# A scheduler that takes its due times backwards from TensorE's list, with fewer opening transfers and an add moved to ScalarE

## The chip, the cores and the metric

The kernel runs on one core of a Trainium2 chip. The metric is the device time of one execution in microseconds (us), the median of several runs. TensorE (PE) multiplies matrices, VectorE (DVE), ScalarE (ACT) and GpSimd (POOL) work elementwise, and SyncE (SP) issues the DMAs. Each engine executes its own list of instructions in order; between engines they wait on semaphores.

## The reference

33280 tokens (8 sequences of 4160) of width 192 go through a convolution of 7 taps, with weights of each token and head from a softmax, and then through a layer of 768 hidden features, each the largest of three products.

```
w = exp(weight_gen - max(weight_gen, axis=-1))          # 8 heads x 7 taps
w = w / (sum(w, axis=-1) + 1e-09)
x = einsum('bshk,bskhg->bshg', w, x_unf)                # the last 7 tokens, 8 heads of 24
h = maximum(maximum(x @ w1, x @ w2), x @ w3)            # 192 -> 768
return h @ w_out                                        # 768 -> 192
```

All is float32.

## The kernel before

The tokens are cut into 65 chunks of 512 (4 tiles of 128); two chunks make a super, for which x (`xt`) and the tap weights (`wt`) are loaded by one DMA each. For every chunk these steps follow one another:

- *Softmax of a super*: largest of the taps on DVE (L326), difference on POOL (L331), exp on ACT (L335), sum on DVE (L340), the 1e-9 added on DVE (L344), reciprocal on DVE (L348), product on POOL (L352).
- *Taps*: for each tile POOL writes the products (`r`, L370), and DVE sums them over the taps (`acc`, L382).
- *Turning*: features must lie on the partitions. DVE transposes in blocks of 32x32 (L421), and ACT moves the blocks into place with 24 copies per chunk (`room`, L432). The first two chunks are transposed on PE instead (L402).
- *Parts*: x is split in a high part of reduced precision (`xa_hi` L444, `xc` L449 on ACT) and a low part (`xa_lo` L460, `xb` L465), so that products of parts add up to float32.
- *Up*: PE computes x(w2-w1) and x(w3-w1) for six blocks `j` of 128 hidden features, two banks for each `j` (i = 0, 1), 9 matmuls of 512 columns per bank. The array's rows are used as two halves, "L" and "U". For each `j`, ACT takes max(bank, 0) of the first bank (`m`, L859), DVE the larger of that and the second bank (L867), ACT the high part (`h_hi`, L871), and DVE, or POOL for j = 1 and 4, the low part (`h_lo`, L878).
- *Down*: h @ w_out, four banks per chunk (one for each tile) of 30 matmuls, which read `h_hi` and `h_lo` of all six `j` in turn, and `wca`, `wcb`, in which w1 @ w_out is composed (casts on ACT L759, differences on DVE L767). ACT copies half a bank (`ob`, L928), DVE adds (`o`, L935), and a DMA stores the chunk.

On PE the order is written by hand: the "down" of chunk c-1 stands in chunk c behind its j = 0, 1, 2. Both kinds of matmul have line 802. So between two "down"s PE computes j = 3, 4, 5 of one chunk and j = 0, 1, 2 of the next.

The other engines' order comes from a plan (`Plan`). It plays the program through with a cost for each task: whenever an engine is free, it takes from its ready tasks the one with the earliest due time, and the program is then written in that order, which nothing changes later. Before the change a due time is a number given by hand for each task, counted from the chunk's place on PE (`needed`, a period of 21 us) or from PE's own clock of slots.

In the opening the weights are loaded and split too (Abs L573 on ACT, integer steps L579 to L604 on DVE; differences L631, L661 and low parts `wa_lo` L643 and `wb_lo` L673 on POOL; high parts L637 and L684 on ACT), while chunk 0 waits for them. SP issues nearly all DMAs; in the opening four are issued by ACT.

Of the kernel before, what the change touches and what calls it, by code (L numbers as in the profile page):

```python
# [20 lines left out]
class Hold:  # L21


    def __init__(self, pool):
        self.pool, self.users, self.taken, self.tile = pool, 0, False, None


class Task:
    def __init__(self, engine, cost, emit, deps, due, holds, end):
        self.engine, self.cost, self.emit, self.due = engine, cost, emit, due  # L30
        self.holds, self.after = holds, []
        self.end = cost if end is None else end
        self.missing = 0
        for d in deps:
            d.after.append(self)
            self.missing += 1
        for h in holds:
            h.users += 1


class Plan:
# [4 lines left out]
    LATENCY = 0.12  # L46

    def __init__(self, pools):
        self.free = dict(pools)
        self.waiting = {"L": [], "U": []}  # L50
        self.tasks = []

    def add(self, engine, cost, emit, deps=(), due=0.0, holds=(), end=None):
# [3 lines left out]
        if engine in self.FIXED:  # L57
            self.waiting[engine].append(t)
        return t

    def order(self):
        ready, busy, events, done = {}, {}, [], []
        at = dict.fromkeys(self.FIXED, 0)
        for t in self.tasks:
            ready.setdefault(t.engine, [])
            busy.setdefault(t.engine, 0.0)
            if t.missing == 0 and t.engine not in self.FIXED:
                heapq.heappush(ready[t.engine], (t.due, t.n, t))

        def can(t):  # L70
            need = {}
            for h in t.holds:
                if not h.taken:
                    need[h.pool] = need.get(h.pool, 0) + 1
            return all(self.free[p] >= n for p, n in need.items())

        def start(t, now):
            for h in t.holds:
                if not h.taken:
                    h.taken = True  # L80
                    self.free[h.pool] -= 1
# [3 lines left out]
            heapq.heappush(events, (now + t.cost, 0, t.n, t, "free"))  # L85
            heapq.heappush(events, (now + t.end, 1, t.n, t, "given"))
            heapq.heappush(events, (now + t.end + self.LATENCY, 2, t.n, t, "seen"))

        now = 0.0
        while True:  # L90
            for e in ready:
                if busy[e] > now + 1e-9:
                    continue
                if e in self.FIXED:
                    k = at[e]
                    if k < len(self.waiting[e]):
                        t = self.waiting[e][k]
# [16 lines left out]
            while events and events[0][0] <= now + 1e-9:  # L114
                _, _, _, t, what = heapq.heappop(events)
                if what == "given":
                    for h in t.holds:
                        h.users -= 1
                        if h.users == 0:
                            self.free[h.pool] += 1  # L120
                elif what == "seen":
# [9 lines left out]
def lightconv_maxout_kernel(  # L131
# [100 lines left out]
    plan = Plan(counts | {"conv": 3})  # L232
# [26 lines left out]

    def needed(c):  # L260
        return FIRST + PERIOD * c
# [4 lines left out]
    def transfer(cost, emit, deps=(), due=0.0, holds=(), on="SP"):  # L266
        issue = plan.add(on, 0.45, emit, deps, due, holds)
        return plan.add("DMA", cost, lambda: None, [issue], due, holds, end=cost + 2.0)
# [4 lines left out]
    def load_super(s):  # L273
# [3 lines left out]
        due = needed(cs[0]) - 40  # L277

# [10 lines left out]
        w = transfer(0.0005 * n * H * K, weights, (), due, [hw])  # L289
        if a >= PAD:  # L290
            t = [transfer(0.0005 * (n + PAD) * D, tokens, (), due + 0.1, [hx])]
        else:
            z = PAD - a
            zero = plan.add(
                "DVE", 1.1, lambda: pin(nc.vector.memset(buf(hx)[:, :z], 0.0)), (), due, [hx]
            )
            t = [transfer(0.0005 * (n + a) * D, tokens, (), due + 0.1, [hx])]
            for b in range(B):
                on = "ACT" if s == 0 and b % 2 else "SP"

                def rows(b=b, on=on):
                    to = slice(b * PB + 1, (b + 1) * PB)
                    q = nc.scalar if on == "ACT" else nc.sync
                    pin(
                        q.dma_start(
                            out=buf(hx)[to, :z], in_=xf[to.start - 1 : to.stop - 1, NT - z :]
                        )
                    )

                t.append(transfer(0.1, rows, [zero], due + 0.2, [hx], on))  # L310
# [5 lines left out]
    def softmax(s):  # L316
        n = len(supers[s]) * TC
        due = needed(supers[s][0]) - 32
# [8 lines left out]
            [loads[s][0]], due, [hr, hw],  # L327
# [4 lines left out]
            [a], due + 1, [hr, hw],  # L332
# [3 lines left out]
            [b], due + 2, [hw],  # L336
# [4 lines left out]
            [c], due + 3, [hd, hw],  # L341
        )
        e = plan.add(
            "DVE", 0.3, lambda: pin(nc.vector.tensor_scalar_add(part(hd), part(hd), 1e-9)),  # L344
            [d], due + 3, [hd],
        )
        f = plan.add(
            "DVE", 0.6, lambda: pin(nc.vector.reciprocal(part(hd), part(hd))), [e], due + 3, [hd]  # L348
# [4 lines left out]
            [f], due + 4, [hd, hw],  # L353
# [5 lines left out]
    def taps(c):  # L359
# [3 lines left out]
        due = needed(c)  # L363
        sums = []
        for t in range(TC):
            hr = hold("r")

            def product(t=t, hr=hr):
                pin(
# [11 lines left out]
            def total(t=t, hr=hr):  # L381
                pin(nc.vector.tensor_reduce(buf(ha)[:, t], buf(hr), axis=AX.X, op=ALU.add))  # L382

            p = plan.add(
                "POOL", 2.75, product, [ready[s], *loads[s][1]], due - 26 + 3 * t, [hr, hx, hw]
            )
            sums.append(plan.add("DVE", 1.55, total, [p], due - 22 + 3 * t, [hr, ha]))
        return ha, sums

    def blocks(c, ha, sums, wait):  # L390


        due = needed(c)
        if c < ON_TENSOR:
            ba, bb = hold("bank"), hold("bank")
            got = []
            for t in range(TC):
# [7 lines left out]
                got.append(plan.add("L", 0.6, turn, [sums[t], *wait], due, [ba, bb, ha], end=0.9))  # L405
# [4 lines left out]
        def places():  # L410
# [10 lines left out]
            "DVE", 0.97, lambda: pin(nc.vector.transpose(places()[2], buf(ha))), sums, due - 12,  # L421
# [3 lines left out]
        for q, f in enumerate(range(0, D, 32)):  # L425
            for p in range(0, P, 32):

                def move(f=f, p=p):
# [3 lines left out]
                    pin(nc.scalar.copy(to[:, :, p : p + 32], b[p : p + 32, :, f : f + 32]))  # L432

                got.append(plan.add("ACT", 0.296, move, [turned], due - 11 + q, [hv]))
        return [hv], lambda: places()[:2], got

    def parts(c, hs, places, got):
        due = needed(c)
# [5 lines left out]
            "ACT", act(CH), lambda: pin(nc.scalar.copy(buf(ah), places()[0])), of_a, due - 3,  # L444
# [5 lines left out]
                due - 2.5, [k, *hs],  # L450
# [7 lines left out]
        def a_low():  # L458
            pin(
# [3 lines left out]
        def b_low():  # L463
            pin(
# [5 lines left out]
        lo = plan.add(name, cost, a_low, [hi], due - 1.5, [al, ah, *hs])  # L470
        bl = plan.add(name, cost, b_low, cs, due - 1.4, [b, k, *hs])
# [35 lines left out]
    w_due = lambda jp, i: FIRST + 4 * jp + 2 * i  # L507

    a_in, b_in, d_in = {}, {}, {}

    def load_a(jp):
        for i, w in enumerate(words[:3]):
# [8 lines left out]
                (), w_due(jp, 0) - 22, [a_hold(jp)],  # L521
            )

    def load_b(jps):
        got = []
        for i, w in enumerate(words[:3]):
            for odd, h in enumerate(halves):
                got.append(
                    transfer(
                        0.3 * len(jps),  # L530
                        lambda i=i, w=w, odd=odd, h=h: pin(
                            nc.sync.dma_start(  # L532
                                out=raw_b()[h, jps[0] : jps[-1] + 1, i].rearrange(
                                    "p j n w -> p j (n w)"
                                ),
                                in_=w[P:].rearrange("p (j o n) -> p j o n", j=NP, o=2)[
                                    :, jps[0] : jps[-1] + 1, odd
                                ],
                            )
                        ),  # L540
                        (), w_due(jps[0], 0) - 21.5, [hraw[2]],
                    )
                )
        for jp in jps:
# [487 lines left out]
```

## Time and profile before

| | us |
|---|---|
| median of 3 runs | 1441.08 (1439.87 to 1443.25) |
| the profiled execution | 1444.6 |
| its span, first to last instruction | 1442.8 |
| mean granted clock of TensorE | 0.987 |

Durations below are of the profiled execution. In the page's second part the span is cut into 40 slices of 36 us. The first digit of each row is the opening; from the third slice on each row hardly changes.

```profile
PE   2889999999999999999999999999999999999999
DVE  7867777777777787777778777877877677777543
ACT  3547878878877887787788778877888887788773
POOL 6769888778877887887788778778877877787421
PEclk9679999999999999999999999999999999999999
```

A row gives the busy share in tenths; the PEclk row gives the clock that TensorE was granted, in tenths of full speed. Times in a chain, timeline or window count from the start of the span.

### The profile page before, as it was taken

Reading aid. Unit: us, or ns where it says so; the run is one execution under the profiler, and the core shown is the slowest. Engines: PE = TensorE matmul, PEld = TensorE weight load, DVE = VectorE, ACT = ScalarE, POOL = GpSimd, SP = SyncE. Lnnn points to the kernel's source line nnn. Section 1 sums busy time; section 2 is a strip of 40 time slices with the busy share of each in tenths; the row PEclk is TensorE's granted clock in tenths of the full one; section 3 lists DMA queues with packets and bytes.
Section 4 is the critical chain, followed back from the end, with each engine's and each line's share of the span. In section 5 each row is a group of like instructions: output and inputs, shape, how many; then the busy total and the mean of one; then the engine's idle time right before and its main releaser. Section 6 shows DMA issues by size and latency. Waiting matters only on the chain.

```text
span 1442.8 us, 37119 instructions
## 1 busy us (share of the span) xinstructions
PE 1402.0 (97%) x14878; PEld 1366.1 (95%) x14878; DVE 1043.4 (72%) x1433; ACT 1117.3 (77%) x2828; POOL 1104.2 (77%) x609
## 2 busy tenths in 40 slices
PE   2889999999999999999999999999999999999999
PEld 1579999999999999999999999999999999999998
DVE  7867777777777787777778777877877677777543
ACT  3547878878877887787788778877888887788773
POOL 6769888778877887887788778778877877787421
PEclk9679999999999999999999999999999999999999
DMA  7102111111111111111011111101111111110000
GB/s 249 46 1 79 57 68 57 68 68 57 68 46 46 57 68 68 68 57 64 28 57 68 68 68 57 68 25 67 57 68 68 57 68 44 48 57 24 23 21 26
DMA packets 23405, 85.08 MB, mean 59 GB/s; under 512 B 2768, under 2 KB 9544, under 8 KB 19136
## 3 DMA queue, kind: packets, MB, share of 16 engines
q1 hardware_dynamic: 23112, 82.44, 15.5%
q8 instruction: 116, 1.90, 0.5%
q14 instruction: 57, 0.47, 0.1%
q10 hardware_dynamic: 120, 0.28, 0.1%
HBM read 57.15 MB, written 25.56 MB: 57 GB/s over the span
## 4 chain that ended last, share of the span: by engine, by line
PE 95%; POOL 1%; DMA 1%; ACT 1%; SPq 1%; DVE 1%; issue 0%; POOLq 0%
PE bank L802 95%; POOL r L370 1%; DMA xt<-in_x_dram 1%; SPq L532 1%; DVE den L344 0%; ACT room L432 0%; DMA raw<-in_moe_w_dram 0%; SPq L516 0%; PE bank L733 0%; ACT m L859 0%; POOL wa_lo L643 0%; PE bank L731 0%; ACT wb_hi L684 0%; DVE acc L382 0%; ACT bank L573 0%
## 5 line engine op out<-in xcount | busy, mean ns | idle before, releaser
L370 POOL TENSOR_TENSOR r<-xt,wt 128x1344 f32<-128x1344 f32 x260 | 727.1, 2845 | 143.2 <-DVE acc L382 142.9
L802 PE MATMUL bank<-wo,h_hi 64*128 64x384 f32 x3120 | 675.0, 357 | 0.0
L802 PE MATMUL bank<-wo,h_lo 64*128 64x192 f32 x3120 | 603.4, 249 | 0.0
L432 ACT COPY room<-room 32x128 f32<-32x128 f32 x1512 | 448.4, 297 | 79.0 <-DVE room L421 55.9
L802 PEld LDWEIGHTS bank<-wo,h_lo 64*128 64x128 f32 x3120 | 493.0, 188 | 0.0
L802 PEld LDWEIGHTS bank<-wo,h_hi 64*128 64x128 f32 x3120 | 489.2, 186 | 0.0
L802 PE MATMUL bank<-xa_hi,wa_hi 64*128 64x512 f32 x1560 | 479.9, 394 | 6.0 <-ACT wa_hi L637 3.4
L802 PE MATMUL bank<-xa_hi,wa_lo 64*128 64x512 f32 x1560 | 477.9, 390 | 3.4 <-POOL wa_lo L643 3.3
L802 PE MATMUL bank<-xa_lo,wa_hi 64*128 64x512 f32 x1560 | 476.8, 391 | 0.5 <-DVE xa_lo L460 0.5
L382 DVE TENSOR_REDUCE acc<-r 128x192 f32<-128x1344 f32 x260 | 399.8, 1538 | 0.6 <-POOL r L370 0.3
L859 ACT ACTIVATE m<-bank 128x512 f32<-128x512 f32 x390 | 234.5, 601 | 71.4 <-PE bank L802 66.7
L935 DVE TENSOR_TENSOR o<-bank,ob 128x192 f32<-128x192 f32 x260 | 92.4, 356 | 268.7 <-ACT ob L928 268.5
L802 PE MATMUL bank<-xb,wb_hi 64*128 64x512 f32 x780 | 284.5, 390 | 0.3 <-DVE xb L465 0.3
L802 PE MATMUL bank<-xc,wb_hi 64*128 64x512 f32 x780 | 281.1, 390 | 0.2 <-ACT wb_hi L684 0.2
L802 PEld LDWEIGHTS bank<-xa_hi,wa_hi 64*128 64x128 f32 x1560 | 255.3, 186 | 13.5 <-ACT wa_hi L637 4.3
L802 PEld LDWEIGHTS bank<-xa_hi,wa_lo 64*128 64x128 f32 x1560 | 255.3, 186 | 11.2 <-POOL wa_lo L643 5.6
L802 PEld LDWEIGHTS bank<-xa_lo,wa_hi 64*128 64x128 f32 x1560 | 254.9, 187 | 6.4 <-DVE xa_lo L460 1.5
L802 PE MATMUL bank<-xc,wb_lo 64*128 64x512 f32 x780 | 258.0, 389 | 0.0
L867 DVE TENSOR_TENSOR bank<-bank,m 128x512 f32<-128x512 f32 x260 | 179.0, 689 | 42.2 <-PE bank L802 24.3
L878 POOL TENSOR_TENSOR h_lo<-m,h_hi 128x512 fp32r<-128x512 f32 x130 | 171.7, 1321 | 40.0 <-ACT h_hi L871 39.9
L802 PE MATMUL bank<-wca,xa_hi 64*128 64x384 f32 x520 | 183.4, 353 | 0.0
L878 DVE TENSOR_TENSOR h_lo<-bank,h_hi 128x512 fp32r<-128x512 f32 x260 | 172.4, 681 | 11.4 <-ACT h_hi L871 11.2
(79 smaller groups left out, 2012.5 us busy)
## 6 DMA issues: line engine op xcount, KB each, us to landing
xt<-in_x_dram SPq DMA_DIRECT2D x31, 1344.0 KB, 5.8
out_dram<-o SPq DMA_DIRECT2D x64, 384.0 KB, 2.3
wt<-in_weight_gen_dram SPq DMA_DIRECT2D x32, 224.0 KB, 2.6
h_hi<-in_moe_w_dram SPq DMA_DIRECT2D x6, 256.0 KB, 2.9
xt<-in_x_dram SPq DMA_DIRECT2D x1, 1152.0 KB, 5.8
h_lo<-in_moe_w_dram SPq DMA_DIRECT2D x6, 128.0 KB, 4.0
raw<-in_moe_w_dram SPq DMA_DIRECT2D x3, 256.0 KB, 3.6
room<-in_moe_w_out_dram SPq DMA_DIRECT2D x2, 384.0 KB, 6.4
```

Source lines behind the costliest of these rows:

```text
L370: nc.gpsimd.tensor_tensor(buf(hr).rearrange("p (h g) k -> p k h g", g=G), buf(hx)[:, la + t : la + t + K].rearrange("p k (h g) -> p k h g" ...
L382: pin(nc.vector.tensor_reduce(buf(ha)[:, t], buf(hr), axis=AX.X, op=ALU.add))
L432: pin(nc.scalar.copy(to[:, :, p : p + 32], b[p : p + 32, :, f : f + 32]))
L532: nc.sync.dma_start(out=raw_b()[h, jps[0] : jps[-1] + 1, i].rearrange("p j n w -> p j (n w)"), in_=w[P:].rearrange("p (j o n) -> p j o n", ...
L802: ins = nc.tensor.matmul(buf(hb)[:, :n], w()[h], v()[h], start=half == 0 and first, stop=half == 1 and last,)
L859: lambda: pin(nc.scalar.activation(buf(hm), buf(hb), AF.Relu)), [made], due,
L867: lambda: pin(nc.vector.tensor_tensor(buf(keep), buf(hb), buf(hm), op=ALU.max)),
L878: eng.tensor_tensor(buf(hl)[:, j], buf(keep), buf(hh)[:, j].bitcast(F32), op=ALU.subtract)
L935: nc.vector.tensor_tensor(buf(ho)[:, t], buf(hb)[:, :D], buf(hq), op=ALU.add)
```

## The change

Five things change:

1. *Due times.* A task no longer has a due time of its own, except on PE and a few others. `start_by` goes through the tasks backwards: a task must begin before the earliest of its followers, less its own duration and a latency. What PE must have when comes from its list of slots, `clock[0]`.
2. *Costs.* `vec`, `act` and `gps` get other constants; the end of a task lies a `LAG` of its engine behind the time for which it keeps the engine. A room copy is priced at .207 instead of .296, a product at 2.6 instead of 2.75, a sum at 1.455 instead of 1.55, a transpose at .86 instead of .97.
3. *Transfers of the opening.* The first tokens of each sequence need rows of the one before; these were eight DMAs of 15 rows for each of two supers, and are now four strided ones (64, 32, 16 and 8 rows) on SP. The weights' rows beyond 128 come in 6 DMAs instead of 12. The plan lets 8 transfers be under way at once.
4. *The 1e-9* is added on ACT by an activation with a bias.
5. `tokens(c)` and the "up" and "down" calls are written in another form, with the same order on PE.

```diff
-    LATENCY = 0.12
+    LATENCY = 0.1
+
+    LAG = {"DVE": 0.09, "ACT": 0.1, "POOL": 0.05}
...
+    def start_by(self):
+
+        for t in reversed(self.tasks):
+            latest = [a.by - self.LATENCY - t.end for a in t.after]
+            if t.due is not None:
+                latest.append(t.due)
+            t.by = min(latest, default=1e6)
...
-                            heapq.heappush(ready[a.engine], (a.due, a.n, a))
+                            heapq.heappush(ready[a.engine], (a.by, a.n, a))
...
     def vec(n):
-        return 0.15 + 0.00105 * n
+        return 0.062 + 0.00104 * n
     def act(n):
-        return 0.18 + 0.00084 * n
+        return 0.08 + 0.00083 * n
     def gps(n):
-        return 0.1 + 0.0024 * n
-    PERIOD = 21.0
+        return 0.12 + 0.0022 * n
...
-            for b in range(B):
-                on = "ACT" if s == 0 and b % 2 else "SP"
...
+            step = 2
+            while step <= PB:
+
+                def rows(step=step):
+                    to = buf(hx)[step // 2 :: step, :z]
+                    of = xf[step // 2 - 1 :: step, NT - z :][: P // step]
+                    pin(nc.sync.dma_start(out=to, in_=of))
...
         e = plan.add(
-            "DVE", 0.3, lambda: pin(nc.vector.tensor_scalar_add(part(hd), part(hd), 1e-9)),
-            [d], due + 3, [hd],
+            "ACT", 0.25,
+            lambda: pin(nc.scalar.activation(part(hd), part(hd), AF.Copy, bias=1e-9)),
+            [d], None, [hd],
...
-                got.append(plan.add("ACT", 0.296, move, [turned], due - 11 + q, [hv]))
+                got.append(plan.add("ACT", 0.207, move, [turned], None, [hv]))
...
-        begun, before = {}, []
+        begun, before, at = {}, [], clock[0]
...
-                    "LU"[half], slot, emit, [*deps, *(before if first else [])], 0,
+                    "LU"[half], slot, emit, [*deps, *(before if first else [])], at,
                     [hb, *holds], end=end,
                 )
+                at += slot
```

The lines of the instructions after the change: room copy L438 (before L432), `m` L854, `max` L862, `h_hi` L866, `h_lo` L873, sums L389, products L377, transpose L427, matmuls L797, `wca` and `wcb` L754 and L762, the 1e-9 L352.

**The steady part, on ACT.** This is a stretch between two "down"s about the middle of the program, before the change, from the `m` of j = 3 to the `h_hi` of j = 5 and of the next j = 0 (the row of two):

```order
960 L859 ACTIVATE m<-bank 128x512
961 L432 COPY room<-room 32x4x32 x2
962 L859 ACTIVATE m<-bank 128x512
963 L871 CAST h_hi<-bank 128x512
964 L432 COPY room<-room 32x4x32 x3
965 L859 ACTIVATE m<-bank 128x512
966 L432 COPY room<-room 32x4x32 x2
967 L871 CAST h_hi<-m 128x512
968 L432 COPY room<-room 32x4x32
969 L859 ACTIVATE m<-bank 128x512
970 L432 COPY room<-room 32x4x32 x2
971 L871 CAST h_hi<-bank 128x512 x2
```

The same stretch after the change, in every second chunk, behind the `m` of j = 3 (row 953); the last row is the `h_hi` of j = 5:

```order
954 L438 COPY room<-room 32x4x32 x7
955 L854 ACTIVATE m<-bank 128x512
956 L438 COPY room<-room 32x4x32
957 L866 CAST h_hi<-bank 128x512
958 L438 COPY room<-room 32x4x32 x4
959 L854 ACTIVATE m<-bank 128x512
960 L438 COPY room<-room 32x4x32 x4
961 L866 CAST h_hi<-m 128x512
962 L438 COPY room<-room 32x4x32
963 L854 ACTIVATE m<-bank 128x512
964 L438 COPY room<-room 32x4x32 x4
965 L866 CAST h_hi<-bank 128x512
```

Before the change 10 room copies stand between those two instructions, after it 21 in this stretch and 15 in the chunks between. The copies that stood behind the `h_hi` and among the outputs have moved up.

**The same stretch on DVE**, before the change, from the transpose to the two `h_lo` of j = 5 and the next j = 0:

```order
545 L421 STREAM_TRANSPOSE room<-acc 128x768
546 L867 TENSOR_TENSOR bank<-bank,m 128x512
547 L382 TENSOR_REDUCE acc<-r 128x192
548 L878 TENSOR_TENSOR h_lo<-bank,h_hi 128x512
549 L867 TENSOR_TENSOR m<-bank,m 128x512
550 L382 TENSOR_REDUCE acc<-r 128x192
551 L867 TENSOR_TENSOR bank<-bank,m 128x512 x2
552 L382 TENSOR_REDUCE acc<-r 128x192
553 L878 TENSOR_TENSOR h_lo<-bank,h_hi 128x512 x2
```

And after it:

```order
533 L427 STREAM_TRANSPOSE room<-acc 128x768
534 L389 TENSOR_REDUCE acc<-r 128x192
535 L862 TENSOR_TENSOR bank<-bank,m 128x512
536 L389 TENSOR_REDUCE acc<-r 128x192
537 L873 TENSOR_TENSOR h_lo<-bank,h_hi 128x512
538 L862 TENSOR_TENSOR m<-bank,m 128x512
539 L389 TENSOR_REDUCE acc<-r 128x192
540 L862 TENSOR_TENSOR bank<-bank,m 128x512 x2
541 L389 TENSOR_REDUCE acc<-r 128x192
542 L873 TENSOR_TENSOR h_lo<-bank,h_hi 128x512 x2
```

The `max` of j = 5 and of the next j = 0, a sum and the two `h_lo` stand in the same order; one more sum stands ahead of them.

**The end of the opening, on DVE**, where `wca` and `wcb` are made. Before the change:

```order
108 L767 TENSOR_TENSOR wca<-bank,wca 128x192
109 L382 TENSOR_REDUCE acc<-r 128x192
110 L344 TENSOR_SCALAR den<-den 128x64
111 L767 TENSOR_TENSOR wcb<-bank,wcb 128x192
112 L348 RECIPROCAL den<-den 128x64
```

After it:

```order
93 L356 RECIPROCAL den<-den 128x64
94 L762 TENSOR_TENSOR wca<-bank,wca 128x192
95 L347 TENSOR_REDUCE den<-wt 128x64
96 L356 RECIPROCAL den<-den 128x64
97 L762 TENSOR_TENSOR wcb<-bank,wcb 128x192
```

Between `wca` and `wcb` stood a sum of products and the 1e-9; now a sum of the softmax and a reciprocal stand there, and the 1e-9 is on ACT.

More of the change, by code (lines that the diff above doesn't have):

```diff
@@ L45, with add @@
     FIXED = ("L", "U")
-    LATENCY = 0.12
+    LATENCY = 0.1
+    LAG = {"DVE": 0.09, "ACT": 0.1, "POOL": 0.05}
     def __init__(self, pools):
-        self.free = dict(pools)
-        self.waiting = {"L": [], "U": []}
+        self.pools = dict(pools)
+        self.fixed = {"L": [], "U": []}
         self.tasks = []
-    def add(self, engine, cost, emit, deps=(), due=0.0, holds=(), end=None):
+    def add(self, engine, cost, emit, deps=(), due=None, holds=(), end=None):
+        end = cost + self.LAG.get(engine, 0.0) if end is None else end
         t = Task(engine, cost, emit, list(deps), due, list(holds), end)
@@ L57, in add @@
         if engine in self.FIXED:
-            self.waiting[engine].append(t)
+            self.fixed[engine].append(t)
         return t
+    def start_by(self):
[4 more added lines that the diff above has]
+            t.by = min(latest, default=1e6)
     def order(self):
+        self.start_by()
+        free = dict(self.pools)
         ready, busy, events, done = {}, {}, [], []
         at = dict.fromkeys(self.FIXED, 0)
+        users = {h: h.users for t in self.tasks for h in t.holds}
+        taken = set()
         for t in self.tasks:
+            t.missing = t.before
             ready.setdefault(t.engine, [])
@@ L72, in can @@
             for h in t.holds:
-                if not h.taken:
+                if h not in taken:
                     need[h.pool] = need.get(h.pool, 0) + 1
-            return all(self.free[p] >= n for p, n in need.items())
+            return all(free[p] >= n for p, n in need.items())
         def start(t, now):
             for h in t.holds:
-                if not h.taken:
-                    h.taken = True
-                    self.free[h.pool] -= 1
+                if h not in taken:
+                    taken.add(h)
+                    free[h.pool] -= 1
             t.start = now
@@ L84, in start @@
             busy[t.engine] = now + t.cost
[L85 to L87 removed]
+            heapq.heappush(events, (now + t.cost, 0, t.n, t))
+            heapq.heappush(events, (now + t.end, 1, t.n, t))
+            heapq.heappush(events, (now + t.end + self.LATENCY, 2, t.n, t))
         now = 0.0
@@ L231, in lightconv_maxout_kernel @@
     }
-    plan = Plan(counts | {"conv": 3})
+    plan = Plan(counts | {"conv": 3, "flight": 8})
     def hold(name):
@@ L381, in total @@
             def total(t=t, hr=hr):
-                pin(nc.vector.tensor_reduce(buf(ha)[:, t], buf(hr), axis=AX.X, op=ALU.add))
+                return pin(nc.vector.tensor_reduce(buf(ha)[:, t], buf(hr), axis=AX.X, op=ALU.add))
             p = plan.add(
-                "POOL", 2.75, product, [ready[s], *loads[s][1]], due - 26 + 3 * t, [hr, hx, hw]
+                "POOL", 2.6, product, [ready[s], *loads[s][1]], None, [hr, hx, hw]
             )
-            sums.append(plan.add("DVE", 1.55, total, [p], due - 22 + 3 * t, [hr, ha]))
+            sums.append(plan.add("DVE", 1.455, total, [p], None, [hr, ha]))
         return ha, sums
     def blocks(c, ha, sums, wait):
-        due = needed(c)
         if c < ON_TENSOR:
@@ L403, in turn @@
                     pin(nc.tensor.transpose(buf(bb)[:DB, to], acc[:, t, P:], ident))
-                got.append(plan.add("L", 0.6, turn, [sums[t], *wait], due, [ba, bb, ha], end=0.9))
+                got.append(plan.add("L", 0.6, turn, [sums[t], *wait], clock[0], [ba, bb, ha], end=0.9))
             return [ba, bb], lambda: (buf(ba), buf(bb)[:DB]), got
@@ L420, in blocks @@
         turned = plan.add(
-            "DVE", 0.97, lambda: pin(nc.vector.transpose(places()[2], buf(ha))), sums, due - 12,
+            "DVE", 0.86, lambda: pin(nc.vector.transpose(places()[2], buf(ha))), sums, None,
             [hv, ha],
@@ L424, in blocks @@
         got = []
-        for q, f in enumerate(range(0, D, 32)):
+        for f in range(0, D, 32):
             for p in range(0, P, 32):
@@ L443, in parts @@
         hi = plan.add(
-            "ACT", act(CH), lambda: pin(nc.scalar.copy(buf(ah), places()[0])), of_a, due - 3,
+            "ACT", act(CH), lambda: pin(nc.scalar.copy(buf(ah), places()[0])), of_a, None,
             [ah, *hs],
@@ L580, in single @@
             ),
-            [a], due, [hb],
+            [a], None, [hb],
         )
@@ L733, in turn @@
                 pin(nc.tensor.transpose(b[:, to : to + DB], b32[h, jp, 0], ident[h, h]))
-        got = plan.add("L", 0.5, turn, [one_a[jp], one_b[jp], made, *u_last()], 0, [hb], end=0.8)
+        got = plan.add("L", 0.5, turn, [one_a[jp], one_b[jp], made, *u_last()], clock[0], [hb], end=0.8)
         turned_w[j] = plan.add(
@@ L754, in mult @@
                     )
-            got = plan.add("L", 2.4, mult, deps + u_last(), 0, [hb, hw1t], end=2.8)
+            got = plan.add("L", 2.4, mult, deps + u_last(), clock[0], [hb, hw1t], end=2.8)
             hi = plan.add(
@@ L821, in products @@
         return t
-    clock = [FIRST]
     hs = {}
@@ L951, in down @@
             )
-    made = plan.add("POOL", 1.0, lambda: make_identity(nc, ident), (), -50)
+    made = plan.add("POOL", 1.0, lambda: make_identity(nc, ident), (), 0)
     for s in range(len(supers)):
```

193 lines of the change are left out of this document (87 added, 106 removed).

## Prediction

> **What bounds the kernel now.** I began with the busy shares on the page and the shares by engine of the chain that ended last, then took the longest pieces of that chain in order of time, and last the waits of PE.
>
> ```profile
> span 1442.8 us, 37119 instructions
> PE 1402.0 (97%) x14878; PEld 1366.1 (95%) x14878; DVE 1043.4 (72%) x1433; ACT 1117.3 (77%) x2828; POOL 1104.2 (77%) x609
> ```
>
> ```profile
> 72.73 4.65 PE bank L802 x11
> ...
> 92.22 1347.23 PE bank L802 x12536
> 1439.47 0.33 ACT ob L928
> 1439.82 0.36 DVE o L935
> ```
>
> ```profile
> PE bank L402 <- DVE acc L382: 21.8, 4, 16.6
> PE bank L802 <- DVE wcb L767: 5.2, 1, 5.2
> PE bank L802 <- ACT wa_hi L637: 3.4, 2, 2.7
> PE bank L802 <- POOL wa_lo L643: 3.3, 2, 2.2
> PE bank L802 <- ACT xa_hi L444: 2.3, 2, 1.8
> ```
>
> From 92.22 us on, 12,536 matmuls run without a break, and every wait in the list (total, times, longest) lies in the opening. So two things can change the time: the **opening**, all before 92.22, and a **new wait of PE** in the steady part, where there is none. That ACT, DVE and POOL are three quarters busy means nothing by itself, but each runs its list in order: one late result stops PE.
>
> **The opening.** These are the last steps ahead of the unbroken run: POOL, PE and DVE by the timeline (start, duration) or the chain.
>
> ```profile
> 9.01 10.23 POOL L370 TENSOR_TENSOR r<-xt,wt 128x1344 f32<-128x1344 f32 x4
> ...
> 51.62 2.72 POOL L370 TENSOR_TENSOR r<-xt,wt 128x1344 f32<-128x1344 f32 x1
> 54.14 0.79 POOL L631 TENSOR_TENSOR wx<-wx,w1a 128x256 f32<-128x256 f32 x1
> 54.82 2.71 POOL L370 TENSOR_TENSOR r<-xt,wt 128x1344 f32<-128x1344 f32 x1
> 57.36 0.79 POOL L643 TENSOR_TENSOR wa_lo<-wx,wa_hi 128x256 fp32r<-128x256 f32 x1
> ```
>
> ```profile
> 58.20 6.75 PE bank L802 x23
> ```
>
> ```profile
> 86.33 1.54 DVE L382 TENSOR_REDUCE acc<-r 128x192 f32<-128x1344 f32 x1
> 87.79 4.12 DVE L344 TENSOR_SCALAR den<-den 128x64 f32<-128x64 f32 x1
> 91.82 0.34 DVE L767 TENSOR_TENSOR wcb<-bank,wcb 128x192 fp32r<-128x192 f32 x1
> ```
>
> Chunk 0's "up" ends at 58.20 + 6.75 = 64.95, after the last weight part `wa_lo` of 57.36. By the order, 11 products stand ahead of that `wa_lo` on POOL before the change and 8 after it: 3 x 2.6 us (10.23/4) = 7.8 us less. The first product starts earlier too: DVE's list ahead of the first reciprocal has lost two operations, and the exp's wait for its queue goes, since ACT issues no DMAs there now. I take 2.0 us of the 9.01, between nothing and the 2.6 of one product. The bound is then 9.8 us; walking the new lists with durations from these rows, PE itself being late once, I get 8.9, so "up" of chunk 0 ends near 56 and chunk 1's tail, now at 72.73, near 64.
>
> At the other end the 4.12 us den operation goes from in front of `wcb`. But on ACT 24 room copies now stand between chunk 1's first `m` and the casts of `wca` and `wcb`, where 13 stood (the others were ahead of that `m`). A group of them is quoted below: 4 in 1.22 us, .307 each, so 11 more are 3.4 us. The add on ACT between the two casts waits for DVE's den sum; I put nothing on it. 92.22 - 8.7 - 4.1 + 3.4 = 83. **The opening gives 9 us.** The least is 4 (only the den operation goes), the most 13 (8.7 + 4.1, the rooms hidden).
>
> The other parts are small. The 1e-9 goes 33 times from DVE to ACT:
>
> ```profile
> L344 DVE TENSOR_SCALAR den<-den x33: 181/1186/4124, 7.4 to 1278.4; 128x64 f32<-128x64 f32 x32, 128x32 f32<-128x32 f32 x1
> ```
>
> On ACT no row has this shape; between nothing extra and the 318 ns of an `ob` copy (twice its free size) I take .25, 33 x .25 = 8 us, in places where ACT sat waiting for PE (the .81 us below); uncovered it would be those 8. The transfers merged in the first 27 us count in the 2.0. In the steady part loads and stores keep their sizes, so SP is nothing to the sum.
>
> **The steady part** is where I expect the change to cost. PE runs the "down" of a chunk after three pairs of the next chunk's "up", and in it needs `h_hi` and then `h_lo` of j=5. These rows are ACT, DVE and PE of one such stretch, with idle time and releaser in brackets.
>
> ```profile
> 693.35 0.32 ACT L928 COPY ob<-bank 128x192 f32<-128x192 f32 x1 [0.64 <-PE bank L802]
> 694.48 0.60 ACT L859 ACTIVATE m<-bank 128x512 f32<-128x512 f32 x1 [0.81 <-PE bank L802]
> 696.18 0.92 ACT L432 COPY room<-room 32x128 f32<-32x128 f32 x3 [1.11 <-DVE room L421]
> 697.01 0.57 ACT L871 CAST h_hi<-bank 128x512 fp32r<-128x512 f32 x1
> 697.49 0.58 ACT L859 ACTIVATE m<-bank 128x512 f32<-128x512 f32 x1
> 698.09 0.92 ACT L432 COPY room<-room 32x128 f32<-32x128 f32 x3
> ...
> 702.21 1.08 ACT L871 CAST h_hi<-bank 128x512 fp32r<-128x512 f32 x2
> ...
> 703.81 1.22 ACT L432 COPY room<-room 32x128 f32<-32x128 f32 x4
> ```
>
> ```profile
> 702.21 1.54 DVE L382 TENSOR_REDUCE acc<-r 128x192 f32<-128x1344 f32 x1
> 703.67 1.28 DVE L878 TENSOR_TENSOR h_lo<-bank,h_hi 128x512 fp32r<-128x512 f32 x2
> ```
>
> ```profile
> 704.65 0.25 PE L802 MATMUL bank<-wo,h_lo 64*128 64x192 f32 x1
> ```
>
> Count from the stretch's first `m`, 694.48. The `h_hi` of j=5 starts 7.73 later; its `h_lo` runs 9.19 to 9.85 (half of 1.28); PE reads it at 10.17. So **PE has 0.3 us in hand**. Between that `m` and that `h_hi` stood 10 room copies. In the order after, from about the tenth chunk on, 15 and 21 alternate: 25 stretches of 21, about 33 of 14 or 15.
>
> What a room costs is the crux. Four take 1.22 us (and three .92): starts .307 apart. An `m` behind an `h_hi` starts .48 behind it (697.01, 697.49) though each takes .58: those overlap, rooms don't. The new table prices a room at .207, so its plan puts in rooms that it believes .1 us shorter.
>
> - *15 rooms:* 5 x .307 = 1.54 later: `h_hi` starts at 9.27, ends at 9.85, `h_lo` ends at 10.5. PE wanted it at 10.17: late by .3 to .6, I take .4.
> - *21 rooms:* 11 x .307 = 3.4 later, but there DVE's transpose comes right behind the outputs, and the 1.11 us for it goes: `h_hi` starts at 10.0, ends at 10.6. On DVE the `max` of the next j=0 and a sum (1.46) stand in front of `h_lo`; that `max` waits for an `m` with 17 rooms ahead of it, which ends at 8.8: .7 + 1.46 + .67 brings `h_lo` to 11.65. Late by 1.1 (no sum in front) to 1.8; I take 1.5.
>
> PE issues in order, so a matmul that waits for j=5 stops all behind it, and the next stretch starts from PE's own `m` again: lateness isn't carried over, nor hidden. 25 x 1.5 + 33 x .4 = 37.5 + 13 = **51 us more** (25 x 1.1 = 28 to 25 x 1.8 + 33 x .6 = 65).
>
> The Trainium skill speaks here against my count: "ScalarE: Activation LUTs", section "What ACT_TABLE_LOAD costs", has it that back-to-back ACTIVATEs overlap by about 93 ns, which would put room copies (297 ns) .204 apart. By it the 15 and 21 rooms would take about as long as 10 and 15 do by the rows, and most of the 51 us would be gone; the .48 between `h_hi` and `m` agrees with it, the 1.22 us of four rooms doesn't, and the measurement decides.
>
> **The clock.** A stall also weighs on the granted clock. Windows of the opening (us, busy and instructions of PE, PEld, DVE, ACT, POOL, then the clock):
>
> ```profile
> 39.80:43.20 3.40, 2.45 (x14) 1.39 (x12) 3.40 (x8) 3.33 (x9) 2.62 (x2) 1.00 0.00 0
> 43.20:50.00 6.80, 6.71 (x30) 5.07 (x27) 3.01 (x7) 4.43 (x11) 6.32 (x7) 0.51 0.00 1
> 50.00:53.40 3.40, 2.57 (x14) 1.56 (x10) 3.40 (x6) 2.25 (x5) 3.40 (x3) 0.98 0.02 5
> 53.40:63.70 10.30, 7.14 (x23) 5.47 (x24) 8.33 (x16) 2.49 (x5) 9.33 (x7) 0.51 0.00 0
> ...
> 84.20:87.60 3.40, 2.80 (x17) 2.33 (x15) 2.67 (x4) 1.69 (x5) 3.40 (x3) 1.00 0.00 0
> 87.60:91.00 3.40, 0.00 (x0) 0.00 (x0) 3.40 (x2) 0.00 (x0) 3.40 (x2) 1.00 0.00 0
> 91.00:101.30 10.30, 9.08 (x53) 9.08 (x53) 4.49 (x5) 0.00 (x0) 6.09 (x3) 0.51 0.00 0
> ```
>
> After a window of 3.4 us with .83 or .95 idle the clock was .51; after one with .6 idle it was 1.00. A stall of 1.5 us puts at least .75 into one window, in between. A cold window of 3.4 us loses half, 1.7 us. So it adds 0 (never) to 25 x 1.7 = 43; I take two stalls in three, **29 us**, and none for the short ones.
>
> "TensorE: Matmul & The Clock Gate", section "HAM oscillation", in the Trainium skill puts the danger at idle gaps over about 3.4 us; by it none of these stalls would cool the clock and the 29 us would be 0. The windows at 39.8 and 50.0 speak against it, with PE busy 72 and 76% of each.
>
> **The sum**, against the profiled execution of 1444.6 us (its span and 1.8 around it): 1444.6 - 9 + 51 + 29 = 1515.6. The median shown is 3.5 lower, 1441.08, so I forecast **1512**.
>
> **Rivals.**
> - *No steady wait.* ACT keeps up: .81 and .64 us of idle stand in the quoted rows, and the transpose's 1.11 may go in all stretches. Then only the opening counts: 1441 - 9 = 1432 (1427 to 1437). Against it stand 5 or 11 more copies at .307 and .3 us in hand. It decides at a `h_hi` of j=5 that starts less than 8.1 us behind the stretch's first `m`. The page on ScalarE, taken at its word, gives this case too. This one ends on the other side, faster.
> - *Stalls, but a warm clock:* 1441 - 9 + 51 = 1483 (1460 to 1497).
> - *Every long stall cools it:* 1441 - 9 + 51 + 43 = 1526.
> - *The opening isn't shortened*, since the rooms ahead of `wcb` take back what products and den give: 9 us on any of these; my 1512 becomes 1521.
> - *Small stalls only*, of some .3 us in 30 stretches, cancel the gain: 1441.
>
> **How the numbers follow.** Stalls with at least some cooling .52 (1497 to 1535, the forecast in it); stalls with a warm clock .24; no steady wait .17; cancelled .04; over 1535 .03. A measurement of this kernel can tell about 0.2%, 3 us, from no change: faster .17, same .04, slower .79. To hold 8 in 10 the range must reach into the faster case: **1431 to 1535**; the likeliest case alone has 1497 to 1535.
>
> **What would show it.** Right: PE's waits get lines on L797 behind `h_lo` L873 or `h_hi` L866, some 25 long ones of 1 to 2 us and up to 33 short ones; ACT's groups of rooms still .307 a copy; cold windows behind the long stalls; the unbroken run of PE begins at 83 +- 4. Wrong: the chain has one unbroken run of PE from the opening to the end (no steady wait), or rooms start .2 apart, or stalls stand in front of other things, such as a bank that is not free, which my walk left with slack.

## The result, and the profile after

The changed kernel takes **1514.86 us** (median of 4 runs, 1513.76 to 1515.62), the kernel before, in the same session, 1442.16. The ratio is 1.0505 (95% interval 1.0487 to 1.0523): slower by 5%. The profiled execution took 1513.76, with a span of 1512.0, 69.2 more than the span of before.

First the page of the changed kernel: span, busy shares, and the shares of the chain that ended last.

```profile
span 1512.0 us, 37046 instructions
PE 1437.2 (95%) x14878; PEld 1361.8 (90%) x14878; DVE 1035.3 (68%) x1400; ACT 1126.3 (74%) x2861; POOL 1104.3 (73%) x609
...
PE 74%; ACT 10%; DVE 7%; POOL 4%; issue 2%; DMA 1%; SPq 0%; POOLq 0%; ACTq 0%
```

And the shares of that chain before:

```profile
PE 95%; POOL 1%; DMA 1%; ACT 1%; SPq 1%; DVE 1%; issue 0%; POOLq 0%
```

PE had 95% of that chain and has 74% now; ACT and DVE come into it with 17%, though both are less busy than before as shares. The busy sums of ACT, DVE and POOL changed by 9 us at most. Nobody has much more to do; somebody is late. The waits of PE (engine and line waited for: total, times, longest) name them:

```profile
PE bank L797 <- ACT h_hi L866: 22.3, 27, 1.0
...
PE bank L797 <- DVE h_lo L873: 12.6, 30, 0.4
```

Both lines are new: some 27 breaks of PE's run, each a wait for `h_hi` with one for `h_lo` behind it. The chain of waits around one of them (start, duration, what) shows how such a break is made:

```profile
504.98 1.32 PE bank L797 x11
506.31 0.58 ACT m L854
...
507.84 0.30 ACT room L438
...
508.16 0.62 ACT h_hi L866
508.78 0.20 ACT room L438
508.98 0.50 ACT m L854
...
509.50 0.70 DVE bank L862
510.20 1.45 DVE acc L389
511.65 0.61 DVE h_lo L873
...
512.30 1.84 PE bank L797 x9
```

Read it from the end. PE goes on at 512.30 with `h_lo` of j=5. DVE made that behind a sum (`acc`) and behind the `max` of the next j=0 (`bank`), because its list says so; that `max` waited for an `m`; and on ACT that `m` stood behind four room copies, the `h_hi` of j=4 and one more copy. Between 506.31 and 512.30 PE decides nothing.

Where the 69 us are is read from the stores. These are rows of SP's timeline, after and then before (start of the first of a group, and the number in it); the groups end at the same chunks.

```profile
278.34 23.80 SPq L944 DMA_DIRECT2D out_dram<-o  x2
322.56 25.38 SPq L944 DMA_DIRECT2D out_dram<-o  x2
...
1344.39 157.45 SPq L944 DMA_DIRECT2D out_dram<-o  x8
```

```profile
277.02 21.02 SPq L949 DMA_DIRECT2D out_dram<-o  x2
...
1279.88 152.49 SPq L949 DMA_DIRECT2D out_dram<-o  x8
```

From the first to the last of these rows lie 48 chunks: 1066.1 us after, 1002.9 before, 63.2 more. In steps of two chunks most take 43.94 us where all took 41.79, so one break per two chunks costs 2.15; seven of the 24 steps take some 1.55 more again. Ahead of them the kernel lost 1.3 us net, and behind them 4.7.

Those 1.55 are the clock. The windows here are 3.41 us long, cut on the grid on which the granted clock changed (busy of PE, PEld, DVE, ACT, POOL, then the clock): around the break above, around the next, and around a later one.

```profile
509.25:512.66 3.41, 2.17 (x19) 1.48 (x18) 3.12 (x4) 3.28 (x9) 3.41 (x3) 1.00 0.00 0
512.66:516.08 3.42, 3.42 (x28) 3.42 (x26) 2.31 (x4) 2.49 (x6) 3.42 (x3) 0.50 0.00 0
553.62:557.03 3.41, 2.59 (x27) 2.22 (x24) 2.32 (x3) 3.28 (x10) 3.02 (x3) 1.00 0.01 2
557.03:560.45 3.42, 2.99 (x37) 2.68 (x39) 2.72 (x5) 3.19 (x8) 3.42 (x2) 1.00 0.00 0
```

```profile
952.98:956.39 3.41, 2.18 (x19) 1.49 (x15) 2.75 (x4) 3.28 (x10) 3.41 (x2) 1.00 0.00 0
956.39:959.80 3.41, 3.40 (x45) 3.40 (x47) 2.29 (x4) 3.11 (x7) 3.41 (x3) 1.00 0.02 5
```

The first break fell whole into one window: 1.24 us idle, and the next window ran at half clock. The second was cut by the border into .82 and .43: no change. Two chunks are 12.87 windows long, so the break moves through the window from step to step. From 280 to 1344 us nine windows held a whole break (1.23 to 1.26 us idle): seven were followed by half clock; the one shown last (1.23) and that of 287.38 (1.25) weren't, nor was any window with 1.15 or less. So a whole break lies just at the limit, and what tells the two from the seven isn't shown.

### The profile page after: what moved, and what is told of

Read it like the earlier page. It is cut to its first block, busy times and chain, and to the rows that moved or that the text cites. A ratio compares the mean times of both kernels' runs of the same rounds, so it can differ in the third digit from the quotient of the medians.

```text
span 1512.0 us, 37046 instructions
## 1 busy us (share of the span) xinstructions
PE 1437.2 (95%) x14878; PEld 1361.8 (90%) x14878; DVE 1035.3 (68%) x1400; ACT 1126.3 (74%) x2861; POOL 1104.3 (73%) x609
## 4 chain that ended last, share of the span: by engine, by line
PE 74%; ACT 10%; DVE 7%; POOL 4%; issue 2%; DMA 1%; SPq 0%; POOLq 0%; ACTq 0%
PE bank L797 74%; ACT room L438 5%; DVE acc L389 3%; ACT m L854 3%; POOL r L377 2%; ACT h_hi L866 2%; DVE bank L862 1%; DVE h_lo L873 1%; POOL xb L470 1%; POOL xa_lo L465 1%; DMA raw<-in_moe_w_dram 0%; DVE room L427 0%; DMA xt<-in_x_dram 0%; DMA h_hi<-in_moe_w_dram 0%; POOL h_lo L873 0%
## 5 line engine op out<-in xcount | busy, mean ns | idle before, releaser
L377 POOL TENSOR_TENSOR r<-xt,wt 128x1344 f32<-128x1344 f32 x260 | 711.1, 2820 | 125.1 <-DVE acc L389 122.5
L797 PE MATMUL bank<-wo,h_hi 64*128 64x384 f32 x3120 | 677.3, 361 | 22.4 <-ACT h_hi L866 22.3
L797 PE MATMUL bank<-wo,h_lo 64*128 64x192 f32 x3120 | 608.2, 253 | 12.6 <-DVE h_lo L873 12.6
L797 PEld LDWEIGHTS bank<-wo,h_lo 64*128 64x128 f32 x3120 | 497.4, 191 | 32.1 <-DVE h_lo L873 24.4
L797 PE MATMUL bank<-xa_hi,wa_hi 64*128 64x512 f32 x1560 | 511.8, 396 | 8.7 <-ACT wa_hi L634 8.2
L797 PEld LDWEIGHTS bank<-wo,h_hi 64*128 64x128 f32 x3120 | 488.8, 188 | 27.5 <-ACT h_hi L866 27.5
L797 PE MATMUL bank<-xa_lo,wa_hi 64*128 64x512 f32 x1560 | 509.5, 394 | 1.5 <-POOL xa_lo L465 1.5
L797 PE MATMUL bank<-xa_hi,wa_lo 64*128 64x512 f32 x1560 | 505.3, 391 | 1.4 <-POOL wa_lo L640 1.4
L438 ACT COPY room<-room 32x128 f32<-32x128 f32 x1512 | 448.4, 297 | 58.8 <-DVE room L427 37.6
L389 DVE TENSOR_REDUCE acc<-r 128x192 f32<-128x1344 f32 x260 | 401.5, 1545 | 15.1 <-POOL r L377 13.3
L797 PE MATMUL bank<-xc,wb_hi 64*128 64x512 f32 x780 | 297.0, 389 | 0.0
L797 PE MATMUL bank<-xb,wb_hi 64*128 64x512 f32 x780 | 280.8, 394 | 2.7 <-DVE xb L470 1.8
L797 PEld LDWEIGHTS bank<-xa_hi,wa_hi 64*128 64x128 f32 x1560 | 264.7, 186 | 19.7 <-ACT wa_hi L634 9.8
L854 ACT ACTIVATE m<-bank 128x512 f32<-128x512 f32 x390 | 233.4, 599 | 62.6 <-PE bank L797 57.4
L797 PEld LDWEIGHTS bank<-xa_lo,wa_hi 64*128 64x128 f32 x1560 | 267.5, 186 | 11.6 <-POOL xa_lo L465 2.2
L797 PEld LDWEIGHTS bank<-xa_hi,wa_lo 64*128 64x128 f32 x1560 | 267.2, 187 | 11.3 <-POOL wa_lo L640 2.8
L797 PE MATMUL bank<-xc,wb_lo 64*128 64x512 f32 x780 | 273.6, 390 | 0.0
L873 DVE TENSOR_TENSOR h_lo<-bank,h_hi 128x512 fp32r<-128x512 f32 x260 | 178.9, 688 | 88.6 <-ACT h_hi L866 80.5
L862 DVE TENSOR_TENSOR bank<-bank,m 128x512 f32<-128x512 f32 x260 | 180.6, 695 | 80.3 <-ACT m L854 66.2
L873 POOL TENSOR_TENSOR h_lo<-m,h_hi 128x512 fp32r<-128x512 f32 x130 | 170.4, 1311 | 86.4 <-ACT h_hi L866 86.2
L923 ACT COPY ob<-bank 128x192 f32<-128x192 f32 x260 | 82.2, 317 | 179.5 <-PE bank L797 176.0
```

What stands on the lines that cost most here:

```text
L377: nc.gpsimd.tensor_tensor(buf(hr).rearrange("p (h g) k -> p k h g", g=G), buf(hx)[:, la + t : la + t + K].rearrange("p k (h g) -> p k h g" ...
L389: return pin(nc.vector.tensor_reduce(buf(ha)[:, t], buf(hr), axis=AX.X, op=ALU.add))
L438: return pin(nc.scalar.copy(to[:, :, p : p + 32], b[p : p + 32, :, f : f + 32]))
L797: ins = nc.tensor.matmul(buf(hb)[:, :n], w()[h], v()[h], start=half == 0 and first, stop=half == 1 and last,)
L854: lambda: pin(nc.scalar.activation(buf(hm), buf(hb), AF.Relu)), [made], due,
L862: lambda: pin(nc.vector.tensor_tensor(buf(keep), buf(hb), buf(hm), op=ALU.max)),
```

## The experiments

Each was run beside the kernel before; its median there was 1442 to 1443 us. Four questions were asked.

### Is it the price of a room copy?

The changed kernel with one number other:

```diff
-                got.append(plan.add("ACT", 0.207, move, [turned], None, [hv]))
+                got.append(plan.add("ACT", 0.307, move, [turned], None, [hv]))
```

> The changed kernel with one number other: the plan prices a room copy at .307 us instead of .207. In its order 15 and 10 copies stand ahead of the h_hi of j=5 where 21 and 15 stood; DVE's order in that stretch is the same. Theory (the copies that the plan believes .1 us too short make the h_hi of j=5 late): PE has no break in the steady part, two chunks take 41.8 us again, and only the shorter opening is left: 1432 to 1438 us. Rival (the due times counted backwards, or the sum that now stands ahead of h_lo on DVE, make the wait, whatever a copy is priced at): breaks stay, over 1480 us.

Measured: **1453.83 us**, ratio 1.0081 (1.0061 to 1.0100). 61 of the 73 us are gone with that number, so the price decides; but the theory had 1432 to 1438, and a rest is left. PE's waits and the chain at one of them:

```profile
PE bank L797 <- DVE h_lo L873: 12.6, 26, 0.6
```

```profile
571.15 0.62 ACT h_hi L866
...
571.79 0.30 ACT room L438
...
572.12 0.61 ACT m L854
...
572.75 0.70 DVE bank L862
573.45 1.40 DVE acc L389
574.85 0.66 DVE h_lo L873
...
575.55 1.52 PE bank L797 x11
```

The wait for `h_hi` is gone, the wait behind `max` and the sum has stayed in the chunks with 15 copies: two chunks take 42.50 us, .71 more than before. The same stretch with 10 copies has no break.

The counter-test puts the price into the kernel before, whose due times are set by hand:

```diff
-                got.append(plan.add("ACT", 0.296, move, [turned], due - 11 + q, [hv]))
+                got.append(plan.add("ACT", 0.207, move, [turned], due - 11 + q, [hv]))
```

> The kernel before with one number other: a room copy priced at .207 instead of .296, due times still by hand. Its order puts 14 copies ahead of the h_hi of j=5 in nearly every chunk. Theory: 14 is about what the changed kernel has in its chunks without a break, so no break or one of some .1 us: 1440 to 1448 us. Rival (each copy over 10 costs .3 us): 4 x .307 less .3 us in hand is .9 us in 55 chunks, 1490 us.

Measured: **1494.54 us**, ratio 1.0363 (1.0341 to 1.0386). The theory was wrong, 14 copies aren't free there, and the rival has the size. PE waits for `h_lo` 27 times, up to 1.0 us each, 21.0 in all, and two chunks take 43.5 us instead of 41.79. So the wrong price alone, without the backward due times, makes 52 of the 73 us.

But the rival's mechanism, .9 us in each of 55 chunks from the copies ahead of `h_hi`, isn't what the trace shows. The listed waits come in every second chunk, and this is DVE ahead of one of them (PE goes on at 510.45):

```profile
507.64 0.70 DVE L867 TENSOR_TENSOR bank<-bank,m 128x512 f32<-128x512 f32 x1 [1.36 <-ACT m L859]
508.25 1.54 DVE L382 TENSOR_REDUCE acc<-r 128x192 f32<-128x1344 f32 x1
509.71 1.28 DVE L878 TENSOR_TENSOR h_lo<-bank,h_hi 128x512 fp32r<-128x512 f32 x2
```

The `max` of the next j=0 (first row) waited for an `m` that stood behind copies, a sum followed, and only then came `h_lo`, though the `h_hi` of j=5, begun at 508.26, ended some .9 us ahead of it. So here the copies reach PE by way of DVE's list. And no count of copies is free or dear by itself: in the changed kernel the chunks with 15 had no break.

### Is it DVE's list?

In e5 and e6 the plan lets DVE wait when a more urgent task will be ready before the one at hand would end, which puts the `h_lo` of j=5 ahead of the `max` of j=0:

```diff
+                        if e in ("DVE",) and any(
+                            s.missing and s.by < x[0] and s.seen < now + x[2].cost - 0.1
+                            for s in soon[e]
+                        ):
+                            kept.append(x)
+                            break
                         start(x[2], now)
```

(`soon` holds the tasks whose forerunners have all started, `seen` is when the last of them will be seen to end.) With the price of .207:

> The changed kernel, room copies still priced at .207, but the plan lets DVE wait instead of starting a task when a more urgent one will be ready before it ends. In its order the h_lo of j=5 stands ahead of the max of the next j=0 in every chunk, and 15 copies stand ahead of the h_hi of j=5 in every chunk. Theory after the first runs (PE waits for DVE, where the max of j=0 and a sum stand ahead of h_lo of j=5, and that max for an m that stands behind room copies): no break in the steady part, 1430 to 1442 us. Rival (only the copies ahead of the h_hi of j=5 count, .3 us for each over 10, less .3 in hand): 1.2 us in 55 chunks, 1500 us.

Measured: **1470.02 us**, ratio 1.0199 (1.0179 to 1.0219), between the two. Two chunks take 42.43 us. The chain at a break is now shorter:

```profile
506.63 0.29 ACT room L452
...
506.95 0.60 ACT m L868
507.55 0.48 ACT h_hi L880
...
508.06 0.70 DVE h_lo L887
...
508.80 1.23 PE bank L811 x9
```

With `max` and sum out of the way, the `h_hi` of j=5 itself is late behind the copies, by .6 us per two chunks. Both halves are real: the copies make `h_hi` late, and DVE's list makes it worse. The chunk behind this one, with the same 15 copies, has no break: there ACT waited .60 us for DVE's transpose and not 1.22, and `h_hi` began 8.61 us behind the stretch's first `m`, not 9.22. By the store of 328.96 us the kernel was 10 us behind the one before, lost in the early chunks; their order changed too, and what in it costs the time isn't shown.

With the price of .307:

> The same rule for DVE, with room copies priced at .307: 10 copies ahead of the h_hi of j=5 in every chunk, h_lo of j=5 ahead of the max of j=0. Theory: the waits of .6 us in every second chunk that were left at the price of .307 go, two chunks take 41.8 us, and what is left is the opening, 12 us shorter there: 1427 to 1434 us. Rival (those waits come from the sum in front of h_lo, which stands there still): 1445 to 1455 us.

Measured: **1436.71 us**, ratio 0.9966 (0.9955 to 0.9977). The breaks of .6 us are gone, as the theory had it: from 253 us on PE runs without one.

```profile
253.29 1180.41 PE bank L811 x11192
```

The total is 3 us above the forecast, since the early chunks kept less of the opening's gain: the store of 272.41 us came 4.6 us earlier than in the kernel before, where e1's was 9.4 earlier, at 267.62.

### Do copies overlap if they read the same partitions?

```diff
-        for f in range(0, D, 32):
-            for p in range(0, P, 32):
+        for part in (range(0, P, 32), range(P, D, 32)):
+            for p, f in [(p, f) for p in range(0, P, 32) for f in part]:
```

> The changed kernel with the 24 room copies of a chunk in another sequence, so that consecutive copies read the same 32 partitions and write others, where they read others and wrote the same. The order of everything else is that of the changed kernel, 21 and 15 copies. Theory (a copy takes .307 us from start to start whatever its neighbour reads): 1510 to 1518 us. Rival (two ACT instructions overlap by .1 us, as an m and an h_hi do, if they read the same partitions): copies start .2 us apart, the breaks go, 1432 to 1440 us.

Measured: **1514.70 us**, the same as the changed kernel. The group of seven copies took 2.15 us, .307 from start to start, as there:

```profile
502.36 2.15 ACT L438 COPY room<-room 32x128 f32<-32x128 f32 x7 [0.49 <-DVE room L427]
```

Whether a copy shares the partitions it reads or those it writes with its neighbour doesn't change its price.

### What moved the opening?

The 1e-9 alone, in the kernel before, on ScalarE:

```diff
-            "DVE", 0.3, lambda: pin(nc.vector.tensor_scalar_add(part(hd), part(hd), 1e-9)),
+            "ACT", 0.25, lambda: pin(nc.scalar.activation(part(hd), part(hd), AF.Copy, bias=1e-9)),
```

> The kernel before with the 1e-9 added on ScalarE, all else as it was. Theory: it takes the 4.1 us operation from in front of wcb and nothing else, so PE's unbroken run begins some 4 us earlier: 1436 to 1439 us. Rival (the rooms or another step are late next): within 1 us of before, 1441. Second rival (ACT's order tears: the add stands ahead of an m and waits for DVE): slower by up to .5 us in 32 supers, 1455.

Measured: **1436.79 us**, ratio 0.9961 (0.9950 to 0.9973). PE's unbroken run begins at 84.89 instead of 92.22 us, 7.3 earlier. That is more than the theory had, and not by its mechanism alone: 4.1 of it stand already at chunk 1's tail (68.64 for 72.73), ahead of the 4.1 us operation, since the plan's order of the opening moved too; 3.2 come behind it. By the medians the gain is 6 us. And back on DVE in the changed kernel (with a cost of 1.1 in the plan):

> The changed kernel with the 1e-9 back on DVE. Order: still 21 and 15 copies ahead of the h_hi of j=5, so the theory expects the same breaks; the opening may lose up to 4 us: 1513 to 1522 us. Rival (the add on ACT is what makes ACT late): breaks go, below 1460 us.

Measured: **1512.05 us**, ratio 1.0484 (1.0464 to 1.0504). The breaks stay, 22.1 us for `h_hi`; the operation in front of `wcb` took 1.58 us there, not 4.12, and the early chunks came out a little better. So the 1e-9 has no share in the loss, and in the new order next to none in the gain.

Then a version without breaks in the steady part, with the copy priced above what it takes (`0.40` in the same line):

> The changed kernel with a room copy priced at .40, more than it takes: 7 and 8 copies ahead of the h_hi of j=5, and the m of the next j=0 early. Theory: that m comes early enough for DVE's max and sum, so no break: 1429 to 1438 us. Rival (with copies moved behind the outputs the x parts of the next chunk come late, and PE waits for xa_hi or xb instead): breaks in front of xb or xa_lo, 1445 us or more.

Measured: **1434.83 us**, ratio 0.9956 (0.9939 to 0.9972): faster than both kernels, than the one before by 7 us. The chain has one piece from 279 us to the end:

```profile
279.38 1151.55 PE bank L797 x11246
```

On it the rest of the opening was tried. The early chunks at .307 (`0.307 if c < 6 else 0.40`):

> The changed kernel with a room copy priced at .307 in the first six chunks and at .40 behind them. Theory: the early chunks keep the opening of the price of .307 (first store 13.5 us ahead of the kernel before), the rest has no break as at .40, so it is 2 to 4 us faster than .40 throughout: 1430 to 1433 us. Rival (the early chunks lose what the opening gains whatever they are priced at, since POOL's products bound them): the same as .40, 1434 to 1436 us.

Measured: 1436.71 us, ratio 0.9964 (0.9950 to 0.9978). That is nearer the rival: the first store came at 96.27 instead of 98.06 with .40, and by the store of about 270 us it was 2 us behind. That POOL's products are the reason isn't shown.

The weights' rows beyond 128 in 12 transfers again (`load_b([0])`, `load_b([1, 2])`, as in the kernel before):

> The kernel with a room copy at .40 and the weights' rows beyond 128 in 12 DMAs as before the change, not 6. Theory (the merged ones are 192 KB each and stand on the queues ahead of the other weights, so that PE waits 6.7 us for wa_hi where it waited 2.7 at most): the first up matmul comes 2 to 3 us earlier and the end 1 to 3 us: 1432 to 1434 us. Rival (fewer issues are worth more than the earlier weights, or chunk 0 is bound by POOL behind it): 1434 to 1437 us.

Measured: **1434.71 us**, ratio 0.9943 (0.9922 to 0.9965). The first "up" matmul came 5.75 us earlier, at 22.93 instead of 28.68 (with .40), and the first store 2.0; the median is the same within its spread, as the rival had it. In the profiled executions, though, the 2.0 us were kept to the end (spans of 1432.3 and 1434.2 us), so whether they are a gain stays open.

The first rows in transfers of 15 again:

> The kernel with a room copy at .40 and the first rows of the sequences in 8 DMAs of 15 rows each again, for the first super on two queues. Theory (the first product waits 2.3 us and more for the strided transfers, which land later than the small ones): the first product comes up to 2 us earlier, but the first up matmul waits for weights anyway: 1433 to 1436 us. Rival (the merged rows are what shortens the opening): 1437 to 1441 us.

Measured: 1437.38 us, ratio 0.9960 (0.9947 to 0.9973). The first product came at 11.30 instead of 9.19, later and not earlier: my expectation had the wrong sign. By the first store .4 us of it were left (98.48 and 98.06), and the spans differ by .3 (1434.5 and 1434.2) where the medians differ by 2.6, so what the merged rows are worth isn't settled.

Both together with the mixed price:

> Room copies at .307 in the first six chunks and .40 behind them, and the weights' rows beyond 128 in 12 DMAs. If both help by themselves, 1428 to 1432 us; if only one does, 1432 to 1435 us.

Measured: 1436.20 us, ratio 0.9961 (0.9947 to 0.9974), above both expectations. The five versions from e8 on lie within 3 us of each other. The order of chunks 2 to 8 can take back a lead, as in e9; what bounds these chunks stays open.

## Why the prediction came out right, point by point

The forecast was 1512, the time 1514.86. The mechanism is the one described: copies priced .1 us too short stand ahead of the `h_hi` of j=5, and PE stops at j=5 of a "down". That the number is this close is luck, though: the long breaks cost 14 us more than I had and the opening, with the early chunks behind it, 10 more, while the short breaks cost 13 less and the clock 18 less.

- **What a room copy takes, right.** .307 from start to start, also with another sequence (2.16 us for seven in the changed kernel, 2.15 in e7). The page "ScalarE: Activation LUTs" of the Trainium skill (section "What ACT_TABLE_LOAD costs") has it that back-to-back ACTIVATEs overlap by about 93 ns; that doesn't hold for these copies, which by this figure would take 1.5 us for seven (an estimate).
- **The long breaks, right in kind, too small in size.** I took 1.5 us, with 1.8 as the upper end; measured 2.15 for each two chunks. `h_hi` of j=5 began 10.52 us behind the stretch's first `m`, not 10.0: I had dropped the whole wait for DVE's transpose, and .49 of it stayed. `h_lo` ended at 12.04, not 11.65. 24 steps of 2.15 are 52 us, not 37.5 for 25. These rows have the first `m`, the wait and that `h_hi`:

```profile
500.22 0.60 ACT L854 ACTIVATE m<-bank 128x512 f32<-128x512 f32 x1 [0.76 <-PE bank L797]
501.31 2.16 ACT L438 COPY room<-room 32x128 f32<-32x128 f32 x7 [0.49 <-DVE room L427]
510.74 0.59 ACT L866 CAST h_hi<-bank 128x512 fp32r<-128x512 f32 x1
```

- **The short breaks, wrong.** I had 33 of .4, 13 us; there are none. These are ACT's first `m` and first copies, and DVE's `h_lo` of j=5, of a stretch with 15 copies in the changed kernel:

```profile
524.70 0.60 ACT L854 ACTIVATE m<-bank 128x512 f32<-128x512 f32 x1 [0.72 <-PE bank L797]
525.97 1.53 ACT L438 COPY room<-room 32x128 f32<-32x128 f32 x5 [0.67 <-DVE room L427]
```

```profile
534.13 0.69 DVE L873 TENSOR_TENSOR h_lo<-bank,h_hi 128x512 fp32r<-128x512 f32 x1 [0.81 <-ACT h_hi L866]
```

  `h_lo` began 9.43 us behind the first `m` and ended in time, since the transpose came .44 earlier (.67 us of waiting, not the 1.11 that I used), and no `max` of j=0 stands ahead of `h_lo` in that list. E1 and e5 have breaks with 15 copies: the count says nothing without DVE's list and the time at which its transpose comes.
- **The clock, right in kind, too large.** I took two breaks in three, 29 us; it was seven in 24, 7 x 1.55 = 11 us. The limit that I read from the opening's windows, between .6 and .83 us of idle time, doesn't hold: in the steady part windows with up to 1.15 idle stayed warm. Idle time by the profile isn't the whole measure either. In the kernel before, the window from 63.69 to 67.10 us, among those that the prediction's table leaves out, has PE busy throughout, its last 2.2 us with transposes, and half clock came behind it all the same. The rule of "TensorE: Matmul & The Clock Gate" (section "HAM oscillation") in the Trainium skill, which sees the danger from gaps of about 3.4 us, would have had no cold window in the steady part; 1.24 us idle in a window were enough here, seven times.
- **The opening, right at its end, not in what follows.** PE's work behind `wcb` begins at 85.01, 7.2 us earlier (I had 9, to 83): chunk 1's tail came at 67.14 for 72.73, 5.6 earlier where I had 8.7, and the steps behind it gave 1.6 where I had .7. The merged transfers didn't give their 2.0: the first product came at 8.53 instead of 9.01, having waited 2.26 for the new strided rows, and the first "up" matmul came later, 28.27 instead of 26.33. And by the store of 278 us the 7.2 had become a loss of 1.3: 8.5 us were lost in the early chunks, where the chain runs through POOL's products and ACT's copies. That term wasn't in the sum at all. It hangs on the price as well: in e1, with the price alone changed, the store that came at 278.34 here came at 267.62.
- **The 1e-9 on ACT, right**: .257 us each (I had .25; an `ob` copy has three times its free size, not twice), and e4 shows it has no part in the loss.

The sum as measured: 85.01 for 92.22 is -7.2, early chunks +8.5, 24 steps of 2.15 = 51.6 and their cold windows and roundings 11.6, and 4.7 behind the last row: 69.2.

The rival that ended on the faster side wanted a `h_hi` that starts less than 8.1 us behind the first `m`. E8, at the price of .40, is that case: 1434.83, near its 1432.

## What to carry to other kernels

A scheduler with deadlines takes the slack that its table of costs shows. In this kernel a price a third too low for ScalarE's most frequent instruction cost 52 us with due times by hand, while all the rest of the change, at a price of .40, gained 7; check such a price as start to start, in a group of the same instruction, and not as duration less an overlap seen elsewhere. Where an engine with one list serves both the bound engine and the background, look at what stands ahead of the urgent result on each engine of the chain, here the copies on ACT and also the `max` and sum on DVE. After a win in the opening, compare the stores some chunks later: what starts earlier may only wait longer.

## What the runs showed of the hardware

A PE break of 2 us shows as less in the list of waits (.82 for `h_hi` and .42 for `h_lo` around 512 us), since matmuls that have begun count as busy: ahead of that break those of one half start .23 us apart and count .39 each. The period of the stores is the better measure. Whether a break cools the clock depends on where it falls in a grid of 3.41 us: the same break, cut by the grid, cost nothing more, and whole in one window, in seven cases of nine, 1.55 us. And with four strided transfers of 64 to 8 rows the first product came 2 us earlier than with eight of 15 rows (9.19 in e8 and 11.30 in e11), though it waited for them in both; that is so in this order of the plan, as the kernel before had it at 9.01 with eight.
